# One tile for each column piece of w_in, and a new order of steps

## The chip, the cores and the metric

The kernel runs on one core of one Trainium2 chip. The core has five engines that run beside each other, each with its own queue of instructions: TensorE (PE, matrix products; the loading of its stationary operand is shown apart as PEld), VectorE (DVE), ScalarE (ACT), GpSimd (POOL) and SyncE (SP, which here only issues DMA transfers). An engine takes its instructions in order; an instruction that waits holds up all that stand behind it on that engine.

The metric is the device time of one execution in microseconds (us). Before the change three runs gave 194.6, 195.93 and 196.33 us, with a median of 195.93 us.

## The reference

Two parts follow each other. The first is a recurrent layer over 4 batches, 8 heads and 768 time steps of 48 channels; the second is a feed-forward layer of width 2048 on its output.

```python
f = 1 / (1 + exp(-f_logit))
for t in range(768):                    # per batch and head
    state = f[t][:, None] * state + outer(k[t], v[t])     # 48 x 48
    y[t]  = q[t] @ state
x = y.transpose(0, 2, 1, 3).reshape(3072, 384)
h = x @ w_in                            # 384 x 2048
out = maximum(0.01 * h, h) @ w_out      # 2048 x 384
```

All inputs and the output are float32. The kernel works in bfloat16 on TensorE and keeps the running state in float32.

## The kernel before

**Units.** Time is cut into 6 chunks of 128 steps. A *pair* `j` (0 to 11) is one chunk of two batches; a *unit* `a` (0 or 1) is one of the two batches. Each unit gives 128 rows of `x`. Pairs 2c and 2c+1 are chunk c, so pair j needs the state that pair j-2 left.

**Steps.** All work is cut into named steps, and one long text, `order`, lists them. A step's name carries pair, unit and part, as in `uu_0_1_2`. The loop at the end of the kernel calls the functions in that order, so the text fixes the order of instructions on each engine. Each step puts its work on one engine, so two neighbouring words on different engines do not wait for each other unless data or a buffer binds them. The steps that matter here:

- `Lf`, `Lk`, `Lq`, `Lv` (SP, line 98): load a unit's f_logit, k, q or v, one DMA of 192 KB each. There are six buffers for pairs.
- `gate`, `dec` (ACT): logarithm of the forget gate, and the decays. `cs` (PE): running sums by a triangular matrix.
- `k`, `q` (DVE for early pairs, POOL later): k and q times decays. `tk`, `tq` (PE) turn them, `ck`, `cq` (DVE) copy them out of PSUM.
- `v` (POOL): v to bfloat16. `sc` (PE): scores. `mk` (DVE): causal mask. `mx` (PE): y, transposed. `xt` (DVE): y into `xT`, the operand of the feed-forward layer.
- `pt` (PE), `sf` (DVE), `sb` (POOL): update of the state.
- `uu_j_a_g` (PE, line 289) with `pu` (ACT, line 294): block g of 512 columns of `x @ w_in` for one unit, 12 matmuls (4 column groups by 3 slices `kk` of the 384 rows), then the leaky maximum. From pair 4 on `up_j_g` (line 276) and `pr` (line 282) do 256 columns for both units.
- `dn_j_a_r` (PE, line 299): quarter r of the product with w_out. `ob` (DVE): copy out. `st` (SP, line 312): store. The last unit's `dp`, `op`, `sp` do the same in two column parts.

**Weights.** `W_piece` (POOL) issues one DMA that also converts to bfloat16. Pieces 0, 1 and 2 are the columns 0 to 511, 512 to 1023 and 1024 to 2047 of w_in (line 111), pieces 3 to 6 are quarters of w_out (line 115). Ahead of the first one, a one-element copy (line 108) on POOL reads the v of pair 1, unit 0, so that no weight is asked for before that load has landed. The matmul of column group `ff` takes every fourth column of its block:

```python
w_in_b = const.tile([128, NK, FF], BF16, tag="w_in")                   # NK = 3, FF = 2048
...
w_in_b[:, kk, columns(ff)]            # columns(ff): 512c+a to 512c+512, step 4
```

So a block of 512 columns lies in one piece: block 0 in piece 0, block 1 in piece 1, blocks 2 and 3 in piece 2. In the one tile a piece occupies, in each partition, three stretches that lie 2048 elements apart.

**Waits.** No wait is written by hand. The framework derives, from the parts of tiles that instructions read and write, which instruction has to wait for which, and puts semaphores there.

**Hold.** `H_4` (line 128) issues a DMA of a few bytes on SP that reads the second quarter of w_out. SP waits there until that quarter has landed, and the loads of pairs 2 and later stand behind it.

Of the kernel before, what the change touches and what calls it, by code (L numbers as in the profile page):

```python
# [15 lines left out]
def kernel(  # L16
# [85 lines left out]
    w_in_cols = ((0, FF // 4), (FF // 4, FF // 2), (FF // 2, FF))  # L102

    def weights(piece, x, j, a):

        if (x, j, a) not in seen:
            seen.add((x, j, a))
            nc.gpsimd.tensor_copy(out=gate_w[:, 0:1], in_=raw(j, "fkqv"[x])[0:1, a, H - 1, D - 1:D])
        if piece < 3:
# [1 line left out]
            nc.gpsimd.dma_start(out=w_in_b[:, :, lo:hi], in_=moe_w_in[:, lo:hi].rearrange("(k p) n -> p k n", p=128))  # L111
        else:
            n = NF // 4
            part = piece - 3
            nc.gpsimd.dma_start(
                out=w_out_b[:, part * n:(part + 1) * n, :],
                in_=moe_w_out[part * n * 128:(part + 1) * n * 128, :].rearrange("(p a) n -> p a n", a=n))
# [152 lines left out]

    def up(j, g):
        pm = st[j]["pm", g] = ps_m.tile([128, 2, 256], FP32, name="pm", tag="pm")
        for i in range(2):
            ff = 2 * g + i
            for kk in range(NK):
                nc.tensor.matmul(pm[:, i, :], w_in_b[:, kk, columns(ff)],  # L276
# [7 lines left out]
    def up_unit(j, a, g):  # L284
        pm = st[j]["pu", a, g] = ps_m.tile([128, 4, 128], FP32, name="pm", tag="pm")
        for i in range(4):
            ff = 4 * g + i
            for kk in range(NK):
                nc.tensor.matmul(pm[:, i, :], w_in_b[:, kk, columns(ff)], st[j]["xT"][:, kk, a, :],  # L289
# [58 lines left out]
    Lf_0_0 Lk_0_0 Lq_0_0 Lv_0_0 Lf_0_1 gate_0_0 Lk_0_1 Lq_0_1 cs_0_0 dec_0_0 Lv_0_1 v_0_0 Lf_1_0 q_0_0 k_0_0 tq_0_0  # L348
    gate_0_1 Lk_1_0 cq_0_0 Lq_1_0 cs_0_1 tk_0_0 dec_0_1 Lv_1_0 pt_0_0 ck_0_0 sf_0_0 v_0_1 Lf_1_1 sc_0_0 q_0_1 gate_1_0
    Lk_1_1 k_0_1 tq_0_1 mk_0_0_0 Lq_1_1 tk_0_1 mk_0_0_1 cs_1_0 Lv_1_1 cq_0_1 pt_0_1 dec_1_0 ck_0_1 mx_0_0 W_0_3_1_0  # L350
    sf_0_1 sc_0_1 W_1_3_1_0 xt_0_0 gate_1_1 W_2_3_1_0 mk_0_1_1 q_1_0 cs_1_1 W_3_3_1_0 dec_1_1 v_1_0 mk_0_1_0 tq_1_0
    k_1_0 v_1_1 q_1_1 tk_1_0 mx_0_1 cq_1_0 tq_1_1 sb_0_0 ck_1_0 xt_0_1 sc_1_0 k_1_1 W_4_3_1_0 W_5_3_1_0 cq_1_1 tk_1_1
    uu_0_0_0 mk_1_0_1 W_6_3_1_0 ck_1_1 uu_0_1_0 pu_0_0_0 mk_1_0_0 pu_0_1_0 sc_1_1 mx_1_0 uu_0_0_1 xt_1_0 uu_0_1_1
    mk_1_1_0 pu_0_0_1 mk_1_1_1 pt_1_0 pu_0_1_1 uu_1_0_0 mx_1_1 pu_1_0_0 uu_1_0_1 xt_1_1 pu_1_0_1 uu_0_0_2 uu_0_1_2
    pu_0_0_2 pt_1_1 pu_0_1_2 uu_0_1_3 uu_0_0_3 pu_0_1_3 dn_0_0_0 pu_0_0_3 uu_1_0_2 H_4 Lf_2_0 dn_0_1_0 pu_1_0_2 Lk_2_0
    uu_1_1_0 Lq_2_0 dn_0_1_1 dn_0_0_1 uu_1_0_3 dn_0_0_2 Lv_2_0 pu_1_0_3 dn_0_1_2 pu_1_1_0 Lf_2_1 dn_0_0_3 uu_1_1_1
    gate_2_0 Lk_2_1 ob_0_0 dn_0_1_3 sf_1_0 pu_1_1_1 st_0_0 uu_1_1_2 ob_0_1 cs_2_0 sf_1_1 Lq_2_1 dn_1_0_0 dec_2_0
    dn_1_1_0 v_2_0 st_0_1 uu_1_1_3 k_2_0 sb_0_1 Lv_2_1 gate_2_1 q_2_0 tk_2_0 dn_1_0_1 ck_2_0 Lf_3_0 pu_1_1_2 tq_2_0
    pt_2_0 dn_1_1_1 cq_2_0 pu_1_1_3 Lk_3_0 sf_2_0 sc_2_0 cs_2_1 Lq_3_0 mk_2_0_0 dn_1_1_2 dec_2_1 mk_2_0_1 dn_1_0_2
    Lv_3_0 mx_2_0 k_2_1 v_2_1 Lf_3_1 dn_1_0_3 xt_2_0 sb_1_0 tk_2_1 q_2_1 gate_3_0 Lk_3_1 uu_2_0_0 ck_2_1 tq_2_1  # L360
    pu_2_0_0 cs_3_0 Lq_3_1 cq_2_1 uu_2_0_1 dec_3_0 ob_1_0 sc_2_1 Lv_3_1 uu_2_0_2 mk_2_1_0 pu_2_0_1 q_3_0 st_1_0
    dn_2_0_0 k_3_0 pu_2_0_2 sb_2_0 pt_2_1 mk_2_1_1 gate_3_1 tq_3_0 Lf_4_0 tk_3_0 dn_1_1_3 sf_2_1 v_3_0 dn_2_0_1 Lk_4_0
    ck_3_0 cq_3_0 cs_3_1 sb_1_1 Lq_4_0 mx_2_1 dec_3_1 sc_3_0 xt_2_1 dn_2_0_2 Lv_4_0 v_3_1 k_3_1 uu_2_1_0 q_3_1 Lf_4_1
    ob_1_1 tk_3_1 pu_2_1_0 uu_2_1_1 mk_3_0_0 st_1_1 gate_4_0 uu_2_0_3 mk_3_0_1 pt_3_0 Lk_4_1 ck_3_1 mx_3_0 pu_2_0_3
    sf_3_0 tq_3_1 pu_2_1_1 dn_2_1_0 Lq_4_1 cq_3_1 xt_3_0 uu_2_1_2 Lv_4_1 sc_3_1 pu_2_1_2 cs_4_0 Lf_5_0 mk_3_1_1
    dn_2_1_1 dec_4_0 mk_3_1_0 uu_3_0_0 Lk_5_0 gate_4_1 mx_3_1 k_4_0 q_4_0 Lq_5_0 dn_2_1_2 xt_3_1 sb_2_1 pu_3_0_0
    cs_4_1 Lv_5_0 dn_2_0_3 dec_4_1 uu_3_1_0 ob_2_0 Lf_5_1 tk_4_0 q_4_1 pu_3_1_0 pt_3_1 uu_3_1_1 ck_4_0 st_2_0 gate_5_0
# [5 lines left out]
    ck_5_1 dn_3_0_2 cq_5_1 Lk_7_0 pr_4_0 sc_5_2 gate_6_0 up_4_1 Lq_7_0 mk_5_1_0 dn_3_0_3 mk_5_0_1 Lv_7_0 pr_4_1 up_4_2
    mk_5_0_0 Lf_7_1 dn_3_1_3 mk_5_1_1 pr_4_2 up_4_3 Lk_7_1 pt_5_0 mx_5_2 pr_4_3 Lq_7_1 up_4_4 xt_5_0 Lv_7_1 cs_6_0
    sf_5_0 pr_4_4 up_4_5 ob_3_0 Lf_8_0 sb_5_0 dec_6_0 cs_6_1 up_4_6 ob_3_1 st_3_0 pt_5_1 pr_4_5 sb_4_0 dn_4_0_0 sf_5_1
    pr_4_6 up_4_7 st_3_1 xt_5_1 dec_6_1 v_6_0 dn_4_0_1 Lk_8_0 up_5_0 pr_4_7 q_6_0 Lq_8_0 dn_4_0_2 gate_7_0 up_5_1
    Lv_8_0 dn_4_0_3 k_6_0 Lf_8_1 pr_5_0 tq_6_0 ob_4_0 cs_7_0 pr_5_1 tq_6_1 Lk_8_1 up_5_2 cq_6_0 dec_7_0 sb_4_1 cq_6_1
# [61 lines left out]
```

## Time and profile before

| | |
|---|---|
| median of three runs | 195.93 us |
| profiled execution, its own time | 195.9 us |
| span of its instructions | 194.1 us |
| PE busy | 173.9 us, 90% of the span |
| PEld busy | 138.1 us, 71% |
| ACT, DVE, POOL busy | 98.8, 97.5, 75.1 us |
| DMA queue of the loads and stores | 23.60 MB, 57.1% of 16 engines |
| DMA queue of the weights | 3.15 MB, 9.0% of 16 engines |

Times in the views count from the first instruction. In a timeline row the columns are start, busy time, engine, line, operation, output, inputs, shapes and count; in brackets stands the idle time of the engine ahead of it and what ended it. In a row of stretches come the stretch, then for PE, PEld, DVE, ACT and POOL the busy time with the number of instructions, then the granted clock, the DMA share and GB/s. A row on the landing of DMAs gives the shortest, the middle and the longest time from issue to landing in its group.

### The profile page before, as it was taken

The page shows a single profiled execution, that of the slowest core. Times are in us where ns is not written, and L with a number is a line of the kernel's source. Part 1 is how long each engine was busy: PE and PEld are TensorE (multiplying, and loading weights), DVE is VectorE, ACT ScalarE, POOL GpSimd, SP SyncE. Part 2 cuts the span into 40 slices and gives each one's busy share as a digit, 9 for nine tenths or more (in the row PEclk, how much of TensorE's full clock was granted, in tenths as well). Part 3 has the DMA queues.
Part 4 walks back from the last instruction along what each step waited for, and adds up shares of the span by engine and source line. Part 5 has one row for each costly group of instructions (what it writes and reads, how often), then busy time and mean ns, then how long its engine had stood idle before and what let it go on. Part 6 is the DMA issues. An engine that isn't in the chain of part 4 may idle for free.

```text
span 194.1 us, 5638 instructions
## 1 busy us (share of the span) xinstructions
PE 173.9 (90%) x2360; PEld 138.1 (71%) x2360; DVE 97.5 (50%) x212; ACT 98.8 (51%) x201; POOL 75.1 (39%) x138
## 2 busy tenths in 40 slices
PE   0476229999999999999999999999999999999994
PEld 0343128977687888878888778877868888888663
DVE  2398503107688856966347737509737574200131
ACT  4544004726654788544976376974233544644200
POOL 8237060030439089401999373099653040000000
PEclk9999999999999999999999999999999999999999
DMA  6999999934999889979798989991001000021122
GB/s 121 210 197 169 204 195 206 173 75 111 200 213 206 191 160 230 178 171 211 162 239 195 210 184 212 194 244 57 26 19 57 28 5 3 3 78 44 41 81 81
DMA packets 106113, 27.10 MB, mean 140 GB/s; under 512 B 100456, under 2 KB 105192, under 8 KB 106088
## 3 DMA queue, kind: packets, MB, share of 16 engines
q1 hardware_dynamic: 104312, 23.60, 57.1%
q0 software_dynamic: 1776, 3.15, 9.0%
q8 instruction: 18, 0.29, 0.6%
q14 instruction: 7, 0.06, 0.1%
HBM read 25.17 MB, written 4.72 MB: 154 GB/s over the span
## 4 chain that ended last, share of the span: by engine, by line
PE 84%; DMA 8%; SPq 5%; POOL 1%; issue 0%; DVE 0%
PE po L299 31%; PE pm L276 22%; PE pm L289 12%; DMA w_in_b<-in_moe_w_in_dram 6%; PE py L240 5%; PE tp L188 5%; SPq L98 5%; PE pw L207 3%; PE cs L142 2%; DMA v_raw<-in_v_dram 2%; PE pt L251 2%; PE po L321 1%; POOL w_in_b L111 1%; PE cs L145 1%; DVE osb L327 0%
## 5 line engine op out<-in xcount | busy, mean ns | idle before, releaser
L299 PE MATMUL po<-w_out_b,gT 128*128 128x384 bf16 x368 | 71.4, 326 | 0.0
L282 ACT ACTIVATE gT<-pm 128x512 bf16<-128x512 f32 x64 | 37.9, 598 | 38.2 <-PE pm L276 37.5
L276 PE MATMUL pm<-xT,w_in_b 128*128 128x256 bf16 x384 | 51.5, 273 | 0.0
L299 PEld LDWEIGHTS <-gT 128*128 128x128 bf16 x368 | 34.1, 98 | 16.2 <-issue 0.2
L276 PEld LDWEIGHTS <-w_in_b 128*128 128x128 bf16 x384 | 40.7, 114 | 4.6
L212 DVE TENSOR_TENSOR wm<-pw,ut 128x512 bf16<-128x512 f32 x48 | 30.5, 683 | 14.8 <-PE pw L207 14.6
L289 PE MATMUL pm<-xT,w_in_b 128*128 128x128 bf16 x384 | 27.2, 225 | 7.0 <-DMA w_in_b<-in_moe_w_in_dram 7.0
L304 DVE COPY osb<-po 128x384 f32<-128x384 f32 x23 | 12.6, 553 | 37.8 <-PE po L299 36.5
L294 ACT ACTIVATE gT<-pm 128x512 bf16<-128x512 f32 x32 | 18.7, 596 | 24.8 <-PE pm L289 24.5
L289 PEld LDWEIGHTS <-w_in_b 128*128 128x128 bf16 x384 | 24.5, 116 | 9.3 <-issue 6.8
L167 POOL TENSOR_TENSOR qh<-q_raw,a_t 128x384 bf16<-128x384 f32 (+1 forms) x12 | 15.7, 1308 | 23.3 <-ACT a_end L156 15.8
L174 POOL CAST v_b<-v_raw 128x384 bf16<-128x384 f32 (+1 forms) x18 | 11.3, 625 | 33.1 <-DMA v_raw<-in_v_dram 32.3
L246 DVE CAST xT<-py 128x384 bf16<-128x384 f32 x24 | 12.7, 553 | 16.9 <-PE py L240 16.8
L152 ACT ACTIVATE em_t<-cs 128x384 bf16<-128x384 f32 x24 | 11.7, 488 | 12.3 <-PE cs L145 8.7
L261 POOL TENSOR_TENSOR sf<-sf,a_end 128x192 f32<-128x192 f32 x20 | 10.5, 523 | 18.9 <-DVE sf L257 18.6
L264 POOL CAST sb<-sf 64x192 bf16<-64x192 f32 x40 | 14.2, 354 | 5.2 <-PE py L240 2.8
L142 PE MATMUL cs<-lf,ut 128*128 128x384 bf16 x24 | 8.5, 352 | 7.5 <-ACT lf L137 7.5
L136 ACT ACTIVATE e_t<-f_raw 128x384 f32<-128x384 f32 (+1 forms) x18 | 11.3, 629 | 6.4 <-DMA f_raw<-in_f_logit_dram 6.4
L191 DVE COPY kT<-tp 128x512 bf16<-128x512 bf16 x24 | 10.1, 421 | 8.2 <-PE tp L188 8.0
L188 PE MATMUL tp<-ident,qh 128*128 128x128 bf16 x96 | 10.2, 234 | 2.3 <-DVE qh L167 2.2
L153 ACT ACTIVATE a_t<-cs 128x384 bf16<-128x384 f32 x24 | 11.7, 489 | 0.0
L137 ACT ACTIVATE lf<-e_t 128x384 bf16<-128x384 f32 (+1 forms) x18 | 11.4, 631 | 0.6
(46 smaller groups left out, 172.2 us busy)
## 6 DMA issues: line engine op xcount, KB each, us to landing
f_raw<-in_f_logit_dram SPq DMA_DIRECT2D x24, 192.0 KB, 3.8
k_raw<-in_k_dram SPq DMA_DIRECT2D x24, 192.0 KB, 3.8
q_raw<-in_q_dram SPq DMA_DIRECT2D x24, 192.0 KB, 4.0
v_raw<-in_v_dram SPq DMA_DIRECT2D x24, 192.0 KB, 3.9
out_dram<-osb SPq DMA_DIRECT2D x17, 192.0 KB, 2.9
w_out_b<-in_moe_w_out_dram POOLq DMA_DIRECT2D x4, 384.0 KB, 7.5
out_dram<-osb SPq DMA_DIRECT2D x12, 96.0 KB, 1.7
w_in_b<-in_moe_w_in_dram POOLq DMA_DIRECT2D x2, 384.0 KB, 8.1
```

Of the source, the lines that this page charges most:

```text
L142: nc.tensor.matmul(t[:, 0:H * D], ut, lf[:, a, :, 0:D], start=True, stop=True)
L167: eng.tensor_mul(qhs[j % NR][:, a, :, 0:D], raw(j, "q")[:, a], st[j]["a"][:, a].rearrange("t a (h d) -> t a h d", d=D))
L188: nc.tensor.transpose(tp[:, p, :], scaled(j, x)[:, a, 2 * p:2 * p + 2, :], ident)
L212: nc.vector.tensor_mul(wm, st[j].pop(("pw", a, i)), ut[:, None, :].to_broadcast([128, P2, 128]))
L246: nc.vector.tensor_copy(out=xT[:, :, a, :], in_=st[j].pop(("py", a))[:, 0:NK, :])
L264: nc.gpsimd.tensor_copy(out=sb[rows, a, :, i * D:i * D + D], in_=sf[rows, a])
L276: nc.tensor.matmul(pm[:, i, :], w_in_b[:, kk, columns(ff)], st[j]["xT"][:, kk].rearrange("t a s -> t (a s)"), start=(kk == 0), stop=(kk == ...
L282: nc.scalar.activation(gT[:, 2 * g:2 * g + 2, :], st[j].pop(("pm", g)), AF.Prelu, alpha=0.01)
L289: nc.tensor.matmul(pm[:, i, :], w_in_b[:, kk, columns(ff)], st[j]["xT"][:, kk, a, :], start=(kk == 0), stop=(kk == NK - 1))
L294: nc.scalar.activation(gT[:, 4 * g:4 * g + 4, 128 * a:128 * a + 128], st[j].pop(("pu", a, g)), AF.Prelu, alpha=0.01)
L299: nc.tensor.matmul(po, st[j]["g"][:, ff, 128 * a:128 * a + 128], w_out_b[:, ff, :], start=(ff == 0), stop=(ff == NF - 1))
L304: nc.vector.tensor_copy(out=osb, in_=st[j].pop(("po", a)))
```

## The change

The single tile `w_in_b` becomes a list of three tiles, one for each column piece, and the function that picks a stationary operand finds piece and offset. Bytes, shapes, strides of the read columns, number of instructions and DMAs are the same. The text `order` holds the same 820 steps in another order. On SP 17 of 122 steps change place, on POOL 49 of 63, on ACT 24 of 138, on DVE 94 of 183 and on PE 112 of 314, each by five places at most on its engine. All loads up to `Lk_2_1`, `H_4` among them, keep their places on SP.

```diff
-    w_in_b = const.tile([128, NK, FF], BF16, tag="w_in")
+    w_in_cols = ((0, FF // 4), (FF // 4, FF // 2), (FF // 2, FF))
+    w_in_b = [const.tile([128, NK, hi - lo], BF16, name="w_in_b", tag=f"w_in{lo}") for lo, hi in w_in_cols]
...
-            nc.gpsimd.dma_start(out=w_in_b[:, :, lo:hi], in_=moe_w_in[:, lo:hi].rearrange("(k p) n -> p k n", p=128))
+            nc.gpsimd.dma_start(out=w_in_b[piece], in_=moe_w_in[:, lo:hi].rearrange("(k p) n -> p k n", p=128))
...
-    def columns(ff):
+    def w_in(kk, ff):
 
         c, a = divmod(ff, 4)
-        return slice(512 * c + a, 512 * c + 512, 4)
+        piece = [hi > 512 * c for lo, hi in w_in_cols].index(True)
+        lo = 512 * c - w_in_cols[piece][0]
+        return w_in_b[piece][:, kk, lo + a:lo + 512:4]
...
-                nc.tensor.matmul(pm[:, i, :], w_in_b[:, kk, columns(ff)],
+                nc.tensor.matmul(pm[:, i, :], w_in(kk, ff),
...
-                nc.tensor.matmul(pm[:, i, :], w_in_b[:, kk, columns(ff)], st[j]["xT"][:, kk, a, :],
+                nc.tensor.matmul(pm[:, i, :], w_in(kk, ff), st[j]["xT"][:, kk, a, :],
```

The order by engine, at the places that the prediction speaks of (before, then after; other steps between them are left out where there are dots):

```
POOL  v_0_1 W_0 W_1 W_2 W_3 v_1_0 v_1_1 sb_0_0 W_4 W_5 W_6 v_2_0 sb_0_1
      v_0_1 W_0 W_1 sb_0_0 v_1_0 W_2 W_3 W_4 v_1_1 W_5 sb_0_1 W_6 sb_1_0 v_2_0
PE    tk_1_1 uu_0_0_0 uu_0_1_0 sc_1_1 mx_1_0 uu_0_0_1 uu_0_1_1 pt_1_0 uu_1_0_0 mx_1_1 uu_1_0_1 uu_0_0_2 uu_0_1_2
      pt_1_1 uu_0_1_3 uu_0_0_3 dn_0_0_0 uu_1_0_2 dn_0_1_0 uu_1_1_0 dn_0_1_1 dn_0_0_1 uu_1_0_3 dn_0_0_2 dn_0_1_2 dn_0_0_3
      tk_1_1 tq_1_1 uu_0_0_0 uu_0_1_0 sc_1_1 uu_0_0_1 mx_1_0 uu_0_1_1 uu_1_0_0 mx_1_1 uu_1_0_1 pt_1_0 uu_0_0_2 uu_0_1_2
      pt_1_1 uu_0_1_3 dn_0_0_0 uu_1_0_2 dn_0_1_0 uu_0_0_3 dn_0_1_1 dn_0_0_1 uu_1_1_0 uu_1_0_3 dn_0_0_2 dn_0_1_2 dn_0_0_3
SP    H_4 Lf_2_0 Lk_2_0 Lq_2_0 Lv_2_0 Lf_2_1 Lk_2_1 st_0_0 Lq_2_1 st_0_1 Lv_2_1 ... Lk_7_1 Lq_7_1 Lv_7_1 Lf_8_0 st_3_0 st_3_1
      H_4 Lf_2_0 Lk_2_0 Lq_2_0 Lv_2_0 Lf_2_1 Lk_2_1 st_0_0 Lq_2_1 st_0_1 Lv_2_1 ... Lk_7_1 st_3_1 Lq_7_1 Lv_7_1 st_3_0 Lf_8_0
DVE   ... mk_5_1_0 mk_5_0_1 mk_5_0_0 mk_5_1_1 xt_5_0 sf_5_0 ob_3_0 ob_3_1
      ... mk_5_0_0 mk_5_1_0 mk_5_1_1 mk_5_0_1 ob_3_1 sf_5_0 xt_5_0 xt_5_1 ob_3_0
```

From `mx_11_2` on PE has the same order as before.

More of the change, by code (lines that the diff above doesn't have):

```diff
@@ L123, in hold @@
         if piece < 3:
-            hi = w_in_cols[piece][1]
-            src = w_in_b[0:1, NK - 1, hi - 4:hi]
+            src = w_in_b[piece][0:1, NK - 1, 0:4]
         else:
@@ L347 @@
     order = """
[L348 to L367, printed above, removed]
@@ L373 @@
[L373 to L377, printed above, removed]
```

86 lines of the change are left out of this document (55 added, 31 removed).

## The prediction

> **What bounds the kernel now.** I read the page first: busy shares, then the chain that ended last.
>
> ```profile
> PE 173.9 (90%) x2360; PEld 138.1 (71%) x2360; DVE 97.5 (50%) x212; ACT 98.8 (51%) x201; POOL 75.1 (39%) x138
> ...
> PE po L299 31%; PE pm L276 22%; PE pm L289 12%; DMA w_in_b<-in_moe_w_in_dram 6%; PE py L240 5%; PE tp L188 5%; SPq L98 5%; PE pw L207 3%; PE cs L142 2%; DMA v_raw<-in_v_dram 2%; PE pt L251 2%; PE po L321 1%; POOL w_in_b L111 1%; PE cs L145 1%; DVE osb L327 0%
> ```
>
> PE is the bound, and the largest part of the chain that is not PE is a landing of w_in. Where PE's other 10% lie is seen in the view by stretches (columns: PE, PEld, DVE, ACT, POOL).
>
> ```profile
> 14.00:21.30 7.30, 4.75 (x66) 2.80 (x54) 6.59 (x16) 2.17 (x7) 3.93 (x7) 1.00 1.06 177
> 21.30:28.00 6.70, 0.29 (x1) 0.11 (x1) 0.65 (x2) 0.00 (x0) 3.50 (x8) 1.00 1.17 207
> 28.00:40.00 12.00, 11.95 (x188) 10.63 (x189) 2.31 (x4) 6.43 (x11) 0.65 (x2) 1.00 0.97 189
> ...
> 160.00:180.00 20.00, 20.00 (x260) 16.90 (x258) 3.71 (x8) 10.16 (x17) 0.00 (x0) 1.00 0.10 31
> ```
>
> From 28 us PE has no hole that the view shows: the seven stretches from 40 to 180 us, of which the last is quoted, all read 20.00 of 20.00. From 21.3 to 28.0 it runs one matmul. The timeline of PE around that hole:
>
> ```profile
> 21.30 0.30 PE L289 MATMUL pm<-xT,w_in_b 128*128 128x128 bf16 x1 [0.54 <-DMA w_in_b<-in_moe_w_in_dram]
> 28.04 2.62 PE L289 MATMUL pm<-xT,w_in_b 128*128 128x128 bf16 x23 [6.44 <-DMA w_in_b<-in_moe_w_in_dram]
> 30.59 0.61 PE L207 MATMUL pw<-qT,kT 48*128 48x128 bf16 x8
> 31.13 0.30 PE L240 MATMUL py<-wm,v_b 128*32 128x128 bf16 x4
> ...
> 34.29 2.38 PE L289 MATMUL pm<-xT,w_in_b 128*128 128x128 bf16 x36
> 36.50 0.33 PE L251 MATMUL pt<-v_b,kh 128*128 128x96 bf16 x4
> ```
>
> The first of 12 matmuls of `uu_0_0_0` ran at 21.30, the second only at 28.04. Both read block 0, so piece 0 alone. What landed when? The issues of w_in (pieces 0 and 1), the chain's row for piece 2, and the issues of w_out:
>
> ```profile
> L111 POOL DMA_DIRECT2D w_in_b<-in_moe_w_in_dram x2: 786/866/946, 14.2 to 15.2; - x2
> DMA to landing us min/median/max: 7.0/8.1/9.2
> ...
> 15.94 11.96 DMA w_in_b<-in_moe_w_in_dram
> ...
> L115 POOL DMA_DIRECT2D w_out_b<-in_moe_w_out_dram x1: 581/581/581, 16.7 to 16.7; - x1
> DMA to landing us min/median/max: 13.0/13.0/13.0
> ...
> L115 POOL DMA_DIRECT2D w_out_b<-in_moe_w_out_dram x3: 536/548/604, 26.0 to 27.2; - x3
> DMA to landing us min/median/max: 5.5/6.8/8.3
> ```
>
> Issue plus time to landing: piece 0 at 21.2, piece 1 at 15.2 + 9.2 = 24.4, piece 2 at 27.9, and w_out's quarters at 29.7, 31.5, 33.4 and 35.5. The first matmul waited for piece 0, the second for piece 2, whose data it does not read. The code explains it. In the one tile each piece runs, from its first to its last element, across 3 slices of 2048. The operand of slice `kk` = 0 lies before the first element of pieces 1 and 2; that of `kk` = 1 lies inside the extents of all three. If the framework compares extents, `uu_0_0_0` waits for exactly what the trace shows.
>
> **The change, part by part.** *Three tiles.* Each has one writer, so block 0 waits for piece 0 alone. Issue and bytes are the same. The second matmul then follows at 21.41 instead of 28.04 (23 matmuls took 30.59 − 28.04 = 2.55 us, 0.11 each): 6.63 us at most. That counts only if PE has work until 27.9.
>
> *PE's new order* has, ahead of the first reader of piece 2 (`uu_0_0_2`), the same ten steps as before, otherwise sorted. They took from 28.04 to the start of `uu_0_0_2`. That start is inside the run of 36 at 34.29: the next row begins 2.21 us later, 0.74 a dozen, so it was 36.50 − 1.47 = 35.03. That is 6.99 us of work, and from 21.41 it lasts to 28.40, 0.5 us past piece 2. Piece 1 is first read after two `uu` and `sc_1_1`: 21.41 + 2.55 + 0.54 (31.13 − 30.59) = 24.50, 0.1 us after its landing. So the hole fills.
>
> ```profile
> 31.77 0.56 DVE L246 CAST xT<-py 128x384 bf16<-128x384 f32 x1 [9.82 <-PE py L240]
> 32.25 1.28 DVE L212 TENSOR_TENSOR wm<-pw,ut 128x512 bf16<-128x512 f32 x2
> ```
>
> Inside it, `uu_1_0_0` now stands only one `uu` (some 0.7 us) behind `mx_1_0`, and it needs `xt_1_0` from DVE, a copy of 0.56 us. `mx_1_1` needs a mask of 0.64 us queued behind that copy. Both fit to within 0.1 us. I put 0.1 us on each such joint.
>
> *w_out.* Its quarters were first read in these runs: the first at 38.02, the second at 40.66, the third at 42.63 and the fourth two thirds into that run, at 43.9.
>
> ```profile
> 38.02 0.81 PE L299 MATMUL po<-w_out_b,gT 128*128 128x384 bf16 x4
> ...
> 40.66 1.46 PE L299 MATMUL po<-w_out_b,gT 128*128 128x384 bf16 x8
> ...
> 42.63 2.11 PE L299 MATMUL po<-w_out_b,gT 128*128 128x384 bf16 x12
> ```
>
> All come 6.6 us earlier, and ahead of the first two stands one `uu` less (0.7 us): 30.7, 33.4, 36.0 and 37.3, against landings at 29.7, 31.5, 33.4 and 35.5. At least 1 us is to spare.
>
> *POOL* now issues piece 2 after `sb_0_0` and `v_1_0`, and three pieces ahead of `v_1_1`:
>
> ```profile
> 14.22 2.49 POOL L111 DMA_DIRECT2D w_in_b<-in_moe_w_in_dram  x3
> 24.07 0.51 POOL L174 CAST v_b<-v_raw 128x384 bf16<-128x384 f32 x1 [6.04 <-DMA v_raw<-in_v_dram]
> ```
>
> Before, a `v` and an `sb` stood between 24.07 and the next issue at 26.0, so two such steps cost 2 us and piece 2 is issued near 17.9 instead of 15.9. Until 24.4 the queue is busy with pieces 0 and 1, and the landings before were 1.8 to 2.1 us apart per 384 KB whenever they were issued (the quarter issued at 26.0 landed 1.8 us after the one of 16.7). So I expect the same landings. Cost nothing: the queue's backlog hides it. Were that cover gone, piece 2 would land 2 us later, at 29.9, and PE lose 1.5. `v_1_1` waits for its load at 24.07 in any case, behind which pieces 5 and 6 go out by 26.7, before the queue runs dry at 31.5.
>
> *SP.* `H_4` ends with the second quarter of w_out, at 31.5 as before, so six loads do not move while PE does:
>
> ```profile
> 31.56 0.73 SPq L128 DMA_DIRECT2D gate_s<-w_out_b  x1
> ...
> 36.12 1.48 SPq L98 DMA_DIRECT2D f_raw<-in_f_logit_dram  x1
> 37.64 0.78 SPq L98 DMA_DIRECT2D k_raw<-in_k_dram  x1
> 45.37 0.36 SPq L312 DMA_DIRECT2D out_dram<-osb  x1
> ```
>
> After the sixth, SP stood from 38.42 to 45.37 for `st_0_0`, which waits for PE: 6.95 us of room. The store comes at about 38.8, and all later loads move with it. The six are in time:
>
> ```profile
> f_raw<-in_f_logit_dram SPq DMA_DIRECT2D x24, 192.0 KB, 3.8
> ...
> 47.82 0.54 ACT L136 ACTIVATE e_t<-f_raw 128x384 f32<-128x384 f32 x1
> ```
>
> f of pair 2, unit 1 lands near 36.1 + 3.8 = 39.9; its `gate` ran at 47.82 and now is due at 41.2, 1.3 us to spare.
>
> *The order after 40 us.* PE had no idle time there, so a better order could save only what hides in modelled ends. Every step `sc` and `mx` stands about 0.1 us off the one before it:
>
> ```profile
> 61.56 0.83 PE L289 MATMUL pm<-xT,w_in_b 128*128 128x128 bf16 x12
> 62.23 0.39 PE L188 MATMUL tp<-ident,kh 128*128 128x128 bf16 x4
> ...
> 79.39 0.84 PE L289 MATMUL pm<-xT,w_in_b 128*128 128x128 bf16 x12
> 80.16 0.52 PE L240 MATMUL py<-qT,sb 128*32 128x128 bf16 x24
> ```
>
> A dozen takes 0.67 us before a `tp` and 0.77 before a `py`. Both orders have 27 such steps from `uu_0_0_0` on, some 2.7 us that stay. I take zero, with −0.8 and +1.5 as ends: 0.8 is about a third of these joints, and 1.5 is two waits as long as a `uu`.
>
> [...]
>
> *Sum*, on the profiled execution: 195.9 − 6.6 + 0.3 (joints near piece 1, `xt_1_0` and `mx_1_1`) = **189.6 us**; its span would be near 187.8. The median of the runs before is 195.93, so nothing is to be shifted.
>
> **The rivals.** *PE's slow matmuls last longer.* They took 0.111 us in the first 2.55 us after the hole and 0.061 at 34.29. If the slow rate lasted not to about 25 but to 28.3, as small holes could make it, 3.3 us of work would run at 0.111 instead of 0.061: 3.3 × (1 − 0.061/0.111) = 1.5 us, so 191.1. For it: PE was slow before 21.3 at 4.75 of 7.30 us busy. Against it: no hole is left in the walk. The granted clock of 1.00 does not show this slowness. [...]
>
> *Transfers share the queue* instead of landing in order of issue. With three pieces behind it piece 2 would land with the last of them, at 31.5, and PE lose 31.5 − 28.4 = 3.1 us: 192.7. Against it are the even landings.
>
> *The loads become the bound.* They do not follow PE, for instance because the room of 6.95 us is smaller than it looks or a later load is level with its reader:
>
> ```profile
> 120.40 0.84 ACT L136 ACTIVATE e_t<-f_raw 128x768 f32<-128x768 f32 x1 [0.34 <-DMA f_raw<-in_f_logit_dram]
> ```
>
> This `gate` of pair 10 waited for its load, so the stream has no slack there. If it gains only half of the 6.6 us, the time is 192.6; with less, up to 194. Against it: the stores that pace the loads follow PE.
>
> *The wait stays*: `uu_0_0_0` waits for piece 2 for another reason than extents. Then 195.9.
>
> *Slower: a store that was moved forward holds the load queue.* `st_3_1` now stands ahead of `Lq_7_1`, with 34 loads behind it:
>
> ```profile
> 89.46 0.79 SPq L98 DMA_DIRECT2D k_raw<-in_k_dram  x1
> ...
> 86.14 2.48 DVE L212 TENSOR_TENSOR wm<-pw,ut 128x512 bf16<-128x512 f32 x4 [0.91 <-PE pw L207]
> ```
>
> In times of before, SP would reach it at 90.25 (after `Lk_7_1`). Its `ob_3_1` follows the four masks that end at 88.62, plus 0.56 for the copy, so it is ready at 89.2. If it comes over 1 us later, each further us delays all later loads, and by the row at 120.40 PE soon after. It eats the gain at 7.6 us of delay, and the kernel is slower by over 1% from 9.6, at 198 or more. Against it: PE has no waits there.
>
> **How the numbers follow.** About 1%, 1.96 us, is what a measurement of this kernel can tell from no change. Chances: forecast 0.64 (188.8 to 190.4); slow matmuls or small holes 0.15 (to 192.4); shared queue 0.03; loads 0.07; wait stays 0.05; slower 0.06. Faster by over 1%: 0.64 + 0.15 + 0.03 + 0.07 = 0.89; within 1%: 0.05; slower: 0.06. The range begins at the sum less 0.8 for the order and 0.6 for the scatter of runs (those before lay from 194.6 to 196.33), 188.2, and takes in the rivals up to the shared queue, 192.7; it leaves out about half of the loads' case, the wait that stays and the slower case, 0.15.
>
> **What would show it.** In the changed profile `uu_0_0_0` runs its dozen without a hole at 21.3; the wait for w_in after it is under 0.5 us in total; piece 2 lands near 27.9; `gate_s` is issued at 31.6 and the first store near 38.8; ACT and PE are not held by loads; `po` L321 starts near 182. A w_in wait of over 2 us, or PE idle after 30 us, would make the forecast wrong.

## The result and the profile after

Five runs of the changed kernel gave 189.02 to 191.1 us, with a median of 189.98 us; five of the kernel before on the same chip gave a median of 196.07. The ratio is 0.9704, with a 95% interval of 0.9648 to 0.976: the kernel is 3.0% faster. The profiled execution was the slowest of the five, 191.1 us with a span of 189.3.

The page after: its busy line, the chain that ended last, and the DMA issues of w_in with the time to their landing:

```profile
PE 174.3 (92%) x2360; PEld 138.3 (73%) x2360; DVE 98.9 (52%) x212; ACT 98.9 (52%) x201; POOL 76.6 (40%) x138
...
PE po L300 30%; PE pm L277 22%; PE pm L290 12%; PE py L239 5%; SPq L99 5%; PE tp L187 4%; DMA w_in_b<-in_moe_w_in_dram 4%; DMA f_raw<-in_f_logit_dram 3%; PE pw L206 3%; DMA v_raw<-in_v_dram 2%; PE cs L141 2%; PE pt L250 2%; PE po L322 1%; ACT e_t L135 1%; PE cs L144 1%
...
w_in_b<-in_moe_w_in_dram POOLq DMA_DIRECT2D x2, 384.0 KB, 7.8
w_in_b<-in_moe_w_in_dram POOLq DMA_DIRECT2D x1, 768.0 KB, 9.5
```

PE has the same 2360 matmuls and nearly the same busy time (173.9 before); its share rises because the span is shorter. In the chain the landing of w_in fell from 6% to 4%, and a new entry stands there, the landing of f with 3%. Piece 2 (the row of 768 KB) now lands 9.5 us after its issue. The stretches after, in the same columns as before:

```profile
14.00:21.30 7.30, 4.39 (x54) 2.77 (x50) 6.54 (x15) 1.98 (x5) 6.58 (x11) 1.00 1.08 181
21.30:28.00 6.70, 6.12 (x83) 5.50 (x84) 2.30 (x4) 2.26 (x4) 2.94 (x7) 1.00 1.08 187
28.00:40.00 12.00, 12.00 (x169) 9.87 (x167) 2.20 (x6) 6.77 (x13) 0.00 (x0) 1.00 0.95 186
...
60.00:80.00 20.00, 19.80 (x330) 15.74 (x327) 13.92 (x30) 12.01 (x29) 11.81 (x24) 1.00 0.87 183
80.00:100.00 20.00, 19.51 (x256) 15.97 (x256) 10.22 (x23) 14.79 (x31) 12.35 (x18) 1.00 1.00 209
```

Two things are new. From 21.3 to 28.0 PE was busy for 0.29 us and now is for 6.12, so the hole is filled. But in the two stretches from 60 to 100 us, where PE had 20.00 of 20.00, it now lacks 0.20 and 0.49 us. The timeline of PE after, at the start and where those 0.69 us lie:

```profile
21.88 2.75 PE L290 MATMUL pm<-xT,w_in_b 128*128 128x128 bf16 x24 [1.52 <-DMA w_in_b<-in_moe_w_in_dram]
24.57 0.60 PE L206 MATMUL pw<-qT,kT 48*128 48x128 bf16 x8
25.10 1.26 PE L290 MATMUL pm<-xT,w_in_b 128*128 128x128 bf16 x12
26.29 0.24 PE L239 MATMUL py<-wm,v_b 128*32 128x128 bf16 x4
...
29.38 1.51 PE L290 MATMUL pm<-xT,w_in_b 128*128 128x128 bf16 x24
...
77.55 0.40 PE L187 MATMUL tp<-ident,qh 128*128 128x128 bf16 x4 [0.20 <-POOL qh L166]
...
82.60 0.81 PE L277 MATMUL pm<-xT,w_in_b 128*128 128x256 bf16 x6 [0.49 <-ACT gT L283]
```

The two dozens of `uu_0_0_0` and `uu_0_1_0` run as one row without a stop. They start at 21.88, 0.58 us later than the first matmul did before, because piece 0 lands later, at 14.54 + 7.3 = 21.84 against 21.2 (the 1.52 us in brackets). The row of 24 at 29.38 begins with `uu_0_0_2`, the first reader of piece 2; no row behind the first has a wait for w_in.

The two waits of PE go back to loads. The timelines after of ACT, POOL and SP's queue, with the rows that matter:

```profile
80.34 0.85 ACT L135 ACTIVATE e_t<-f_raw 128x768 f32<-128x768 f32 x1 [5.31 <-DMA f_raw<-in_f_logit_dram]
```

```profile
74.32 0.68 POOL L173 CAST v_b<-v_raw 128x384 bf16<-128x384 f32 x1 [3.84 <-PE py L239]
...
76.58 0.91 POOL L166 TENSOR_TENSOR qh<-q_raw,a_t 128x384 bf16<-128x384 f32 x1
```

```profile
32.56 0.73 SPq L127 DMA_DIRECT2D gate_s<-w_out_b  x1
...
37.77 1.69 SPq L99 DMA_DIRECT2D k_raw<-in_k_dram  x1
39.58 0.75 SPq L313 DMA_DIRECT2D out_dram<-osb  x1
...
68.81 0.69 SPq L99 DMA_DIRECT2D v_raw<-in_v_dram  x1
...
74.89 1.08 SPq L99 DMA_DIRECT2D f_raw<-in_f_logit_dram  x1
```

The `gate` at 80.34 is that of pair 6. ACT stood 5.31 us for its load, which was issued at 74.89, and behind it in ACT's queue stood the maximum (`pr`) for which PE waited at 82.60. On POOL the cast of v of pair 5 (issued at 68.81) came at 74.32 after 3.84 us of idle time, and behind it stands the `q` for which PE waited at 77.55. Its row names PE, but in the run with one packed tile (e3, below) the same cast came at 72.47 and names the load, so here too it was likely the load. The SP rows show why loads are tight: the six loads behind `H_4` end at 37.77 + 1.69 = 39.46 and the first store follows at 39.58. Of the 6.95 us for which SP had stood there, 0.12 are left. In the chain after, in order of time, the last product (`po` L322, before L321) starts 188.67 − 183.90 = 4.8 us earlier:

```profile
183.90 2.65 PE po L322 x32
```

The prediction had put it near 182.

### The profile page after: what moved, and what is told of

Same layout as the page of the kernel before. It is cut to its first block, busy times and chain, and to the rows that moved or that the text cites. A ratio compares the mean times of both kernels' runs of the same rounds, so it can differ in the third digit from the quotient of the medians.

```text
span 189.3 us, 5637 instructions
## 1 busy us (share of the span) xinstructions
PE 174.3 (92%) x2360; PEld 138.3 (73%) x2360; DVE 98.9 (52%) x212; ACT 98.9 (52%) x201; POOL 76.6 (40%) x138
## 4 chain that ended last, share of the span: by engine, by line
PE 80%; DMA 9%; SPq 5%; issue 2%; ACT 2%; POOL 1%; DVE 0%; POOLq 0%
PE po L300 30%; PE pm L277 22%; PE pm L290 12%; PE py L239 5%; SPq L99 5%; PE tp L187 4%; DMA w_in_b<-in_moe_w_in_dram 4%; DMA f_raw<-in_f_logit_dram 3%; PE pw L206 3%; DMA v_raw<-in_v_dram 2%; PE cs L141 2%; PE pt L250 2%; PE po L322 1%; ACT e_t L135 1%; PE cs L144 1%
## 5 line engine op out<-in xcount | busy, mean ns | idle before, releaser
L305 DVE COPY osb<-po 128x384 f32<-128x384 f32 x23 | 12.6, 553 | 31.6 <-PE po L300 31.4
L290 PE MATMUL pm<-xT,w_in_b 128*128 128x128 bf16 x384 | 27.6, 227 | 1.5 <-DMA w_in_b<-in_moe_w_in_dram 1.5
L173 POOL CAST v_b<-v_raw 128x384 bf16<-128x384 f32 (+1 forms) x18 | 12.6, 703 | 14.7 <-DMA v_raw<-in_v_dram 8.9
L190 DVE COPY qT<-tp 128x512 bf16<-128x512 bf16 x24 | 10.0, 420 | 10.3 <-PE tp L187 9.8
L255 DVE TENSOR_TENSOR sf<-sf,pt 64x192 f32<-64x192 f32 x20 | 6.8, 342 | 10.5 <-PE pt L250 8.7
```

The source lines that it names most:

```text
L173: nc.gpsimd.tensor_copy(out=vb[:, a], in_=raw(j, "v")[:, a])
L190: nc.vector.tensor_copy(out=turned(j, x)[:, P2 * a:P2 * a + P2, :], in_=st[j].pop(("tp" + x, a)))
L290: nc.tensor.matmul(pm[:, i, :], w_in(kk, ff), st[j]["xT"][:, kk, a, :], start=(kk == 0), stop=(kk == NK - 1))
```

## The experiments

To see where the time lies, I cut each span in three. *Start* is when the first `uu` begins; *ten steps* is from there to the start of `uu_0_0_2`, which both orders reach after the same ten steps; *rest* is what then follows to the end of the span. For the kernel before these are 21.30, 35.03 − 21.30 = 13.73, and 194.1 − 35.03 = 159.07 us. For the kernel after they are 21.88, 29.38 − 21.88 = 7.50, and 189.3 − 29.38 = 159.92. Each profile is one execution, and the median is that of all runs. The ratio is to the kernel before on the same chip; e1 to e4 shared one chip, e5 to e8 another and e9 to e12 a third. Where a diff shows the text `order`, the rest of the lines is left out.

| run | median us | ratio, 95% interval | span | start | ten steps | rest |
|---|---|---|---|---|---|---|
| before | 196.07 | | 194.1 | 21.30 | 13.73 | 159.07 |
| after | 189.98 | 0.9704 (0.9648 to 0.976) | 189.3 | 21.88 | 7.50 | 159.92 |
| e1_tiles_only | 188.11 | 0.9625 (0.9591 to 0.966) | 187.0 | 20.99 | 6.95 | 159.06 |
| e2_order_only | 195.93 | 1.003 (1.0005 to 1.0055) | 194.2 | 20.51 | 14.74 | 158.95 |
| e3_one_tile_packed | 189.67 | 0.9706 (0.9677 to 0.9736) | 187.7 | 20.71 | 8.06 | 158.93 |
| e4_piece2_early | 189.04 | 0.9656 (0.9618 to 0.9693) | 187.5 | 21.59 | 7.01 | 158.90 |
| e5_tiles_hold3 | 188.55 | 0.9659 (0.9604 to 0.9715) | 186.6 | 20.34 | 7.18 | 159.08 |
| e6_piece2_early_gate6 | 189.28 | 0.9695 (0.9649 to 0.9741) | 188.3 | 21.57 | 7.79 | 158.94 |
| e7_new_order_warm | 188.16 | 0.9638 (0.96 to 0.9676) | 186.6 | 20.50 | 7.19 | 158.91 |
| e8_tiles_only_warm | 188.05 | 0.9633 (0.9595 to 0.9671) | 186.3 | 21.09 | 6.18 | 159.03 |
| e9_new_order_fill | 189.17 | 0.9674 (0.9638 to 0.9709) | 186.8 | 21.59 | 6.27 | 158.94 |
| e10_tiles_only_fill | 187.97 | 0.9599 (0.9568 to 0.963) | 185.6 | 20.52 | 6.13 | 158.95 |
| e11_changed_again | 189.3 | 0.9688 (0.9642 to 0.9733) | 188.0 | 20.53 | 7.17 | 160.30 |
| e12_tiles_only_again | 188.45 | 0.9624 (0.9592 to 0.9656) | 186.3 | 20.24 | 6.97 | 159.09 |

My theory was that extents in the one tile make the wait, that the tiles remove it, and that the order is worth nothing. The rivals were that the gain comes from the order, and that a tile, not an extent, is what the framework compares.

### One part at a time

**Tiles without the order.** The kernel after with the old text `order`, nothing else.

```diff
...
-    xt_0_0 W_1_3_1_0 pt_0_1 gate_1_1 q_1_0 sb_0_0 mk_0_1_0 cs_1_1 mk_0_1_1 tq_1_0 dec_1_1 v_1_0 sf_0_1 mx_0_1
-    W_2_3_1_0 k_1_0 k_1_1 tk_1_0 W_3_3_1_0 cq_1_0 W_4_3_1_0 ck_1_0 v_1_1 q_1_1 sc_1_0 xt_0_1 W_5_3_1_0 mk_1_0_0 sb_0_1
+    sf_0_1 sc_0_1 W_1_3_1_0 xt_0_0 gate_1_1 W_2_3_1_0 mk_0_1_1 q_1_0 cs_1_1 W_3_3_1_0 dec_1_1 v_1_0 mk_0_1_0 tq_1_0
...
```

> The three tiles with the order of before. Theory (the tiles alone take the wait away, and the ten steps ahead of the first reader of piece 2 are long enough in the old order too): the first uu runs its dozen without a hole near 21.3, the first reader of piece 2 comes near 28.4 and piece 2 lands near 27.9; 189.3 to 190.5 us, ratio near 0.97, so the new order is worth under 1 us. Rival (the order does the work, since it puts piece 2 behind other POOL steps and sorts the steps for the landings): 192 to 195 us, with w_in waits of 2 us or more.

It ran in 188.11 us, 0.9625 of before. The whole gain is there, and more than the full change brought; the time lies below the 189.3 to 190.5 us that I had expected. PE's timeline in this run:

```profile
20.99 2.75 PE L290 MATMUL pm<-xT,w_in_b 128*128 128x128 bf16 x24 [0.61 <-DMA w_in_b<-in_moe_w_in_dram]
...
27.20 2.38 PE L290 MATMUL pm<-xT,w_in_b 128*128 128x128 bf16 x36
```

There is no hole behind the first matmul. The second dozen of the row of 36, which begins at 27.20 + 0.74 = 27.94, is `uu_0_0_2`.

**The order without the tiles.** The kernel before with the new text `order`, nothing else.

```diff
...
-    sf_0_1 sc_0_1 W_1_3_1_0 xt_0_0 gate_1_1 W_2_3_1_0 mk_0_1_1 q_1_0 cs_1_1 W_3_3_1_0 dec_1_1 v_1_0 mk_0_1_0 tq_1_0
+    xt_0_0 W_1_3_1_0 pt_0_1 gate_1_1 q_1_0 sb_0_0 mk_0_1_0 cs_1_1 mk_0_1_1 tq_1_0 dec_1_1 v_1_0 sf_0_1 mx_0_1
...
```

> The new order with the one tile of before. Theory (the wait is for the last piece and hangs on the tile alone): the second matmul of the first uu waits until piece 2 has landed. In the changed kernel piece 2 was issued at 19.30 and landed 9.5 us later, at 28.8, against 27.9 before; so PE starts about 0.9 us later than before: 196 to 197.5 us. Rival (the order brings part of the gain): 190 to 194 us.

It ran in 195.93 us, a ratio of 1.003. PE's timeline in this run:

```profile
20.51 0.30 PE L289 MATMUL pm<-xT,w_in_b 128*128 128x128 bf16 x1
27.52 2.62 PE L289 MATMUL pm<-xT,w_in_b 128*128 128x128 bf16 x23 [6.71 <-DMA w_in_b<-in_moe_w_in_dram]
```

The hole is whole again, at the same matmul, although the order is the new one. So the order does not touch the wait. The time is just under the expected range: 0.4 us above before on the same chip (195.51), where 0.9 was forecast. That the first matmul (slice `kk` = 0) runs and only the second (`kk` = 1) waits, here as before, also fits extents; if a write in strided stretches counted for the whole tile, the first would have waited too.

**One tile, with the pieces packed one after the other.** The tile is single as before, but a piece now is one contiguous stretch of it, so the extents of the pieces do not overlap.

```diff
-    w_in_b = [const.tile([128, NK, hi - lo], BF16, name="w_in_b", tag=f"w_in{lo}") for lo, hi in w_in_cols]
+    w_in_all = const.tile([128, NK * FF], BF16, name="w_in_b", tag="w_in")
+    w_in_b = [w_in_all[:, NK * lo:NK * hi].rearrange("p (k n) -> p k n", k=NK) for lo, hi in w_in_cols]
```

> The new order and one tile again, but in it each piece lies in one unbroken stretch, piece after piece, instead of three stretches 2048 elements apart. Theory (the framework compares extents of reads and writes inside a tile, and the extents of before overlapped): no wait for piece 2 at the first uu, and the time of the changed kernel, 189 to 191 us. Rival (a wait covers every earlier write of the same tile, so only separate tiles help): the hole of 6 us stays, 196 to 197.5 us.

It ran in 189.67 us, 0.9706, against 0.9704 for the changed kernel. PE's timeline in this run:

```profile
20.71 2.75 PE L291 MATMUL pm<-xT,w_in_b 128*128 128x128 bf16 x24 [0.72 <-DMA w_in_b<-in_moe_w_in_dram]
...
25.62 0.32 PE L240 MATMUL py<-wm,v 128*32 128x128 bf16 x4
25.88 1.76 PE L291 MATMUL pm<-xT,w_in_b 128*128 128x128 bf16 x24
```

There is no hole in one tile, so what is compared are extents and not tiles. That settles the mechanism: the three runs together leave room neither for the order nor for the tile as such. (The last two rows are for later: in this execution PE was still slow at 25.62, 0.32 us for a group that takes 0.23 to 0.24 from 27.57 on.)

**Both again, side by side.** To measure the price of the order on one chip.

```diff
 e11: the kernel after, nothing changed
 e12: the kernel after with the old order, as in e1
```

> The changed kernel itself, on the same chip as the tiles alone, for a direct comparison and a second profile. Theory (the new order costs 0.5 to 1 us in the ten steps, and at times 0.5 to 0.7 us where the gate of pair 6 holds ACT): 189.2 to 190.2 us, 1 to 1.6 us above the tiles alone. Rival (the difference was scatter between chips): within 0.5 us of the tiles alone.

> The three tiles with the order of before once more, beside the changed kernel on one chip. Theory: 187.9 to 188.6 us, the first uu at 20.3 to 21.3, the ten steps 7.0 to 7.2 us, the rest 159.1. Rival: 189 to 190, as the changed kernel.

The medians are 189.3 and 188.45 us. With the first pair, e3 against e1 (189.67 and 188.11, intervals apart; e3 stands for the changed kernel there), the new order costs 0.9 to 1.6 us. In the second pair the intervals overlap a little (one begins at 0.9642, the other ends at 0.9656). The two profiles of that pair differ by 1.7 us of span: 0.29 in the start, 0.20 in the ten steps, where I had expected 0.5 to 1, and 1.21 in the rest. In the profile of e11 the same two waits are seen as after (timelines of ACT and of PE):

```profile
78.96 0.85 ACT L135 ACTIVATE e_t<-f_raw 128x768 f32<-128x768 f32 x1 [5.60 <-DMA f_raw<-in_f_logit_dram]
```

```profile
76.39 0.40 PE L187 MATMUL tp<-ident,qh 128*128 128x128 bf16 x4 [0.72 <-POOL qh L166]
...
81.22 0.82 PE L277 MATMUL pm<-xT,w_in_b 128*128 128x256 bf16 x6 [0.26 <-ACT gT L283]
```

Here ACT stood 5.60 us, PE lost 0.72 + 0.26 = 0.98 us, and the rest is 160.30. In e12 the old order has this `gate` behind `pr_4_0`, ACT did not wait for f there, and PE had no hole (ACT's timeline, then the stretches):

```profile
77.62 0.83 ACT L135 ACTIVATE e_t<-f_raw 128x768 f32<-128x768 f32 x1
```

```profile
60.00:80.00 20.00, 20.00 (x337) 16.39 (x335) 14.24 (x31) 13.31 (x30) 10.75 (x21) 1.00 0.99 202
80.00:100.00 20.00, 20.00 (x259) 16.62 (x257) 11.29 (x27) 13.84 (x29) 15.06 (x23) 1.00 1.03 213
```

The column *rest* says more. Without ACT's long wait it is 158.90 to 158.95 in all six other profiles of a new order, and 158.95 to 159.09 in those of the old one. So in the steady state the new order is worth 0.1 us. What it costs appears in two places: in the rest of both profiles of the changed kernel, and for e3 and e6 in the ten steps (8.06 and 7.79).

### Is it the late landing of the weights?

In the new order POOL issues piece 2 and the first quarters of w_out later. Three runs try that.

**Piece 2 early.** The new order, with pieces 2 and 3 issued straight behind piece 1.

```diff
-    xt_0_0 W_1_3_1_0 pt_0_1 gate_1_1 q_1_0
+    xt_0_0 W_1_3_1_0 W_2_3_1_0 W_3_3_1_0 pt_0_1 gate_1_1 q_1_0
...
-    W_2_3_1_0 k_1_0 k_1_1 tk_1_0 W_3_3_1_0 cq_1_0
+    k_1_0 k_1_1 tk_1_0 cq_1_0
```

> The changed kernel with pieces 2 and 3 issued on POOL straight behind piece 1, as before. In the changed kernel piece 2 landed at 28.8 and the second quarter of w_out near 32.5, about 1 us later than before, and piece 0 at 21.84 against 21.2. Theory (my forecast that the queue's backlog hides the later issue was a little wrong): piece 2 lands near 27.9 and the second quarter near 31.6, the loads start 1 us earlier; as the first reader of piece 2 was not waiting, the gain is at most 0.5 us: 189.3 to 190 us. Rival (the landings do not depend on the issue, the 1 us is scatter between executions): landings at 28.3 to 28.9 again and the same time, 189.5 to 190.5.

It ran in 189.04 us (0.9656), 0.6 us less than e3 on the same chip, with overlapping intervals. POOL's timeline of after, and then the row that groups the issues of w_in in this run (shortest, middle and longest, then first and last start) with its row for piece 2:

```profile
14.54 1.72 POOL L111 DMA_DIRECT2D w_in_b<-in_moe_w_in_dram  x2
...
19.30 0.80 POOL L111 DMA_DIRECT2D w_in_b<-in_moe_w_in_dram  x1
```

```profile
L111 POOL DMA_DIRECT2D w_in_b<-in_moe_w_in_dram x3: 775/788/943, 14.7 to 16.4; - x3
```

```profile
w_in_b<-in_moe_w_in_dram POOLq DMA_DIRECT2D x1, 768.0 KB, 11.2
```

Both asked for piece 0 at nearly the same time (14.54 and 14.66). After issued piece 2 at 19.30 and it landed at 28.8; here it was issued at 16.4 and landed at 27.6. `H_4` ended at 32.56 there and 31.28 here. The second pair that starts alike is e11 and e12 (13.78 and 13.79): piece 2 landed at 18.13 + 9.5 = 27.6 and at 15.50 + 10.7 = 26.2, and `H_4` ended at 32.13 and 29.91. So in these pairs an issue that comes 2.6 to 2.9 us later went with 1.2 to 1.4 us at piece 2 and 1.3 to 2.2 us at `H_4`. But over all profiles the two groups overlap: from the first issue to the landing of piece 2 it is 12.1 to 14.0 us with the early issue (nine profiles, mean 12.8) and 13.0 to 14.3 with the late one (five, mean 13.5). An effect of some 0.7 us is likely and not proved. The time came 0.3 us below the range of my theory, and the landings 0.3 us before those it named.

**The hold on an earlier piece.** The tiles alone, with SP's hold on the first quarter of w_out in place of the second, so that the loads go out earlier.

```diff
-    uu_0_1_3 uu_0_0_3 pu_0_1_3 dn_0_0_0 pu_0_0_3 uu_1_0_2 H_4 Lf_2_0
+    uu_0_1_3 uu_0_0_3 pu_0_1_3 dn_0_0_0 pu_0_0_3 uu_1_0_2 H_3 Lf_2_0
```

> The three tiles with the order of before, and the hold on SP waits for the first quarter of w_out instead of the second, so the loads of pair 2 begin near 29.7 instead of 31.5. Theory (with PE 6.6 us earlier the room of SP is used up, as in the run with the tiles alone, where the first store followed the sixth load by 0.1 us, but no reader waits for a load yet): no gain, 188 to 189.5 us; the last quarters of w_out land up to 1 us later and PE waits under 0.5 us for them. Rival (the load stream has become the bound): 186.3 to 187.3 us, with fewer waits for f on ACT.

It ran in 188.55 us (0.9659), no faster than the tiles alone at 188.11 and 188.45. In the old order the loads behind the hold are not what bounds.

**The gate moved back.** The run with piece 2 early, and `gate_6_0` behind `pr_4_0`, where it stood in the old order.

```diff
-    gate_6_0 ... pr_4_0
+    ... pr_4_0 gate_6_0
```

> The changed kernel with two parts of its order undone: pieces 2 and 3 issued straight behind piece 1, and the gate of pair 6 back behind the first leaky maximum of pair 4 on ACT. In the changed kernel that gate held ACT for 5.31 us until a load had landed, and PE waited 0.49 us for ACT after it. Theory (these two places are what the new order costs against the tiles alone, 1.5 us of time): 188 to 188.6 us, as the tiles alone, and no wait of PE on ACT. Rival (the cost lies elsewhere, in how long PE's slow matmuls last after the start): 188.8 to 189.8, as with pieces 2 and 3 early alone.

It ran in 189.28 us (0.9695) and did not come near the tiles alone. Its rest is 158.94, but that of e4, without the move, is 158.90: in neither profile did ACT wait long for that f (1.65 us in e4, not at all in e6), so the move had nothing to save. What was lost here lies in the start (21.57) and the ten steps (7.79). The theory that the gate explains the whole price of the order fell with this run.

So the price of the order is known as a sum (0.9 to 1.6 us in the two pairs) and not in its parts. Late loads of pairs 5 and 6 are one. For f of pair 6 ACT stood 5.31 and 5.60 us in the two profiles of the changed kernel, where `H_4` ended at 32.1 or later and that f was issued at 74.89 and 74.06. It stood 1.6 to 2.3 us in e3, e4, e7 and e9, where `H_4` ended at 29.8 to 31.3 and f was issued at 71.0 to 72.8. Why the loads were late in just those two is open, since e3 issues the same transfers in the same order.

### What is left in the start

With the hole closed the next cost in the start is that PE runs slowly at first: in the profile after, the 24 matmuls at 21.88 took 2.75 us and the 24 at 29.38 took 1.51. Four runs put matmuls of a constant into PE's gaps; their result is never read.

**From the beginning on.** 56 extra matmuls in the order of e4 (e7, shown; `D_n` is n matmuls), and 53 in the old order (e8: the first two places the same, then `D_10` behind `sc_0_1` and `D_5` behind `tk_1_1`).

```diff
+    def warm(n):
+        po = ps_o.tile([128, KD], FP32, name="po", tag="po")
+        for _ in range(n):
+            nc.tensor.matmul(po[:, 0:128], ident, ident, start=True, stop=True)
...
-    cs_0_0
+    D_26 cs_0_0 D_12
...
-    pt_0_1
+    pt_0_1 D_10
...
-    tq_1_1
+    tq_1_1 D_8
```

> The changed kernel with pieces 2 and 3 early, and 56 extra matmuls of 128 columns on constants, in PE's idle time before the weights land; their result is never read. It takes away the slow stretch after the start of the uu steps. Theory (that stretch lasted 2.9 to 5.2 us by execution and costs half of its length): the first dozen takes 0.7 us instead of 1.3, the ten steps 5.4 us instead of 7.0 to 8.1; PE is then at the first reader of piece 2 by 27 and waits for its landing near 27.9, so 0.5 to 1.2 us are gained on the same kernel without them: 187.8 to 188.5 us. Rival (the stretch is not a matter of earlier work on PE): the first dozen still takes 1.3 us and the time stays at 188.6 to 189.5, or grows by what the extra matmuls delay.

> The three tiles with the order of before, and 53 extra matmuls on constants in PE's idle time at the start, as in the run beside it. Theory: the slow stretch goes, piece 2 becomes the bound of the start, 0.3 to 0.6 us are gained on the tiles alone: 187.4 to 187.9 us, and the same time as the new order with piece 2 early and the same extra matmuls, to within 0.5 us, since the two orders then differ in nothing that binds. Rival (the order of before is better in the rest of the kernel too): over 0.8 us below the run beside it.

They ran in 188.16 and 188.05 us. By ratios, since the chips differ, e7 is 0.0018 below e4 (some 0.35 us) and e8 0.0008 above e1, with overlapping intervals: no gain that can be told. In e8 the ten steps fell from 6.95 to 6.18 us, in e7 not (7.19), so that e7's time lies in the expected range by luck and not by the mechanism, which would have made them 5.4; e8's lies above its range. The two runs differ by 0.11 us, within the expected 0.5: with pieces 2 and 3 early and extra matmuls, no price of the order can be told. The stretches of e7 and PE's timeline in it show that the extra work made PE fast and that this did not last:

```profile
5.00:10.00 5.00, 3.26 (x39) 2.47 (x39) 2.67 (x7) 2.93 (x8) 0.96 (x2) 1.00 1.11 220
10.00:15.00 5.00, 4.19 (x54) 2.82 (x52) 4.79 (x10) 2.52 (x7) 2.55 (x5) 0.54 1.16 222
```

```profile
7.48 0.39 PE L187 MATMUL tp<-ident,kh 128*128 128x128 bf16 x4
...
11.20 0.61 PE L187 MATMUL tp<-ident,kh 128*128 128x128 bf16 x4 [0.17 <-DVE kh L160]
```

The same four matmuls took 0.39 us at 7.48 and 0.61 at 11.20. From 5 to 10 us PE was busy for only 3.26 us, and then the granted clock reads 0.54.

**Only ahead of the first block.** The same matmuls nearer to the first `uu`: ten in the changed kernel (e9, shown), and 29 in the tiles alone (e10: `D_10` behind `sc_0_1`, `D_4` behind `tq_1_0`, `mx_0_1` and `sc_1_0`, `D_2` behind `tq_1_1`, `D_5` behind `tk_1_1`).

```diff
-    tq_1_1
+    tq_1_1 D_10
```

> The changed kernel with 10 extra matmuls on constants on PE between the last step before the weights and the first uu; they fill up to 1.1 of the 0.7 to 1.5 us that PE stood there. From the traces so far a run is three parts: the start of the first uu (20.3 to 21.9 us, set by piece 0), the ten steps to the first reader of piece 2 (old order 7.0 to 7.2, new order 7.0 to 8.1) and the rest (158.9 to 159.1 in both orders, 159.9 in the profile of the changed kernel). Theory (the new order pays in the ten steps, because PE stands idle ahead of them and its slow stretch ends later): ten steps near 7.0 and 0.5 to 1 us under the changed kernel run beside it. Rival (the length of the slow stretch is chance): the same time as the changed kernel to within 0.4 us.

> The three tiles with the order of before, and 29 extra matmuls on constants in every gap of PE from 14.6 us to the first uu, so that PE runs without a stop for about 6 us ahead of it. Theory (without such a stop the slow stretch is over when the weights land): the first dozen takes about 0.7 us, the ten steps about 5.4, PE then waits up to 1 us for piece 2, and the time is 0.5 to 1.2 us under the tiles alone run beside it: 186.9 to 187.7 us. Rival (piece 2's landing, at 26 to 28 us, already decides): no gain over 0.3 us.

e9 ran in 189.17 us, 0.13 less than e11, where 0.5 to 1 was expected: nothing that its interval can tell. PE's timeline shows why:

```profile
20.52 1.27 PE L339 MATMUL po<-ident 128*128 128x128 bf16 x10
21.59 2.13 PE L290 MATMUL pm<-xT,w_in_b 128*128 128x128 bf16 x24
```

The ten steps fell to 6.27 us, 0.9 less than in e11. But piece 0 had landed at 20.5 (issued at 13.95, 6.6 us to landing), and the ten extra matmuls, themselves slow (1.27 us, where five took 0.44 at 20.24 in e10), kept the first `uu` back until 21.59. The gain was spent ahead of it.

e10 ran in 187.97 us, a ratio of 0.9599 (0.9568 to 0.963), the best of all. That is 0.48 us less than e12, and the intervals overlap; I had expected more. PE's timeline:

```profile
18.79 0.40 PE L187 MATMUL tp<-ident,qh 128*128 128x128 bf16 x4
...
20.52 1.50 PE L290 MATMUL pm<-xT,w_in_b 128*128 128x128 bf16 x24
...
22.88 1.53 PE L290 MATMUL pm<-xT,w_in_b 128*128 128x128 bf16 x24 [0.19 <-DMA w_in_b<-in_moe_w_in_dram]
...
26.65 1.53 PE L290 MATMUL pm<-xT,w_in_b 128*128 128x128 bf16 x24 [0.27 <-DMA w_in_b<-in_moe_w_in_dram]
```

PE is fast before the first `uu` begins (0.40 us for the four matmuls at 18.79, which took 0.61 in e1), two dozens take 1.50 us where they took 2.75, and the ten steps are down to 6.13. But now they end before the weights: PE waits 0.19 us for piece 1 and 0.27 for piece 2. So the weights' landing is the next bound, and it leaves little of what a faster start could give.

## Why the prediction was right, step by step

The forecast of 189.6 us for the median stands against 189.98, and the mechanism is shown: extents (e3), the hole without the tiles (e2), and no hole with them (e1). That the number came so close is in part luck: the tiles alone are worth 0.6 to 0.8 us more than the 6.63 forecast, the order, put at zero, takes back 0.9 to 1.6, and the two errors offset each other.

- **The tiles.** A gain of 6.63 us was forecast from the hole, on condition that ten steps fill it. The medians differ by 6.1. For the tiles alone it is 195.51 − 188.11 = 7.4 and 195.64 − 188.45 = 7.2 us, against the kernel before on the same chips. In the profiles, e1's span is 7.1 us shorter than before: 6.78 in the ten steps and 0.31 in the start. No matmul behind the first waits for w_in, as forecast.
- **The start of the first `uu`.** It was taken to stay at 21.30. In the profile after it is 21.88, and over all runs 20.24 to 21.88: it goes with the landing of piece 0 (20.3 to 21.8), except in e8, e9, e10 and e12, where PE itself came later than that. The landing was taken from one execution as if it were fixed.
- **The ten steps.** 6.99 us from the second matmul on, or 7.10 from the first, were forecast; 7.50 came. PE was slow until 26.29, for 4.4 us (a dozen took 1.26 us at 25.10 and 0.86 at 28.51). The rival with slow matmuls, to which 1.5 us were given, thus came true by 0.4 us in this profile and by 1.0 in that of e3; of this, 0.3 had been allowed for in the sum, as joints.
- **POOL at no cost.** Piece 2 was to be issued near 17.9 and to land as before, at 27.9. The steps between took not 2 us but 19.30 − (14.54 + 1.72) = 3.0, so it was issued at 19.30, and it landed at 28.8. "Same landings" failed, by an estimated 0.7 us in the mean. The even 1.8 to 2.1 us per 384 KB on which it rested do not hold between pieces 0 and 1, which landed 24.4 − 21.2 = 3.2 us apart. It cost PE nothing there, since the ten steps ended at 29.38.
- **SP.** `gate_s` came at 32.56 and not at 31.6, the first store at 39.58 and not near 38.8. The room of 6.95 us was as wide as reckoned, and 0.12 us of it remain.
- **ACT and PE are not held by loads.** This is the step that failed. PE lost 0.69 us after 77 us, 0.49 of it to a `gate` that waited 5.31 us for f. The prediction itself named PE idle after 30 us as what would make it wrong. It gave the loads' rival 0.07 with half of the gain lost; it came true with a tenth of it lost. The row it rested on was of pair 10, and the tight load was that of pair 6, whose `gate` the new order had moved ahead of `pr_4_0`; that move was not weighed.
- **The order after 40 us.** Zero, from −0.8 to +1.5, was forecast. The rest is 0.1 us shorter where ACT does not wait, and 0.85 longer in the profile after.
- **The slower rival** did not occur: `st_3_1` was issued at 86.72, 0.1 us behind the load ahead of it. The wait did not stay, and the transfers did not share the queue: piece 2 landed at 28.8, well before `H_4` ended at 32.56.

On the profiled execution the sum closes. The first reader of piece 2 starts at 29.38 where 28.40 was forecast (0.58 from piece 0, 0.40 from the ten steps), and the rest is 0.85 longer; 0.3 was allowed in the sum, for joints in the ten steps. 0.98 + 0.85 − 0.3 = 1.5 us, and the execution took 191.1 where 189.6 was forecast. The median was nearer because that execution was the slowest of five.

The prediction had the gain as one sum of tiles and order, with the order at zero. It could not see that the tiles alone are worth more, 0.9625 against 0.9704 of the time before.

## What to carry to other kernels

When an instruction waits for a transfer whose data it does not read (here for 6.44 us), look at the extents of the pieces in their tile: lay each piece out as one stretch, or give it a tile of its own. Change the layout and the order of work in separate runs; here the layout was worth all of the gain, and the new order took back 0.9 to 1.6 us. With the hole closed, several bounds stood close to each other here (the slow first matmuls, an estimated 1.3 us in e12; the landing of the weights, for which PE waited 0.46 us in e10; the room in the load queue, of which 0.12 us were left), and removing one of them bought little: the median of e10 is 0.48 us below that of e12.
